# Two of three token tiles of a half batch by seven block products instead of eight, with the block sums on GpSimd

## The chip, the cores and the metric

The kernel runs on one core of a Trainium2 chip. The metric is the device time of one execution in microseconds. A core has five engines that work beside each other: TensorE (PE; its weight loads are shown apart as PEld), VectorE (DVE), ScalarE (ACT), GpSimd (POOL) and SyncE (SP), which here only starts transfers.

## The reference

Attention with routing, then a feed-forward layer. Inputs are q, k and v with 4 batches, 8 heads, 768 tokens and 64 dimensions, centroids (8 heads, 16 clusters), w_in (512 x 2048) and w_out (2048 x 512).

```
q_assign = argmax(q_n . c_n);  k_assign = argmax(k_n . c_n)      # q_n, k_n, c_n normalised
scores   = q . k^T / sqrt(64), or -1e9 where q_assign != k_assign
x        = softmax(scores) . v           # heads side by side: (3072, 512)
h        = x @ w_in                      # (3072, 2048)
out      = (h * sigmoid(h)) @ w_out      # (3072, 512), float32
```

## The kernel before, in words

A batch's 768 tokens are split in two half batches (b, c) of 384 tokens, which are three tiles of 128 tokens. Everything is on chip in f16 with sums in f32. Work goes through these steps, and the names are those that the profile shows:

- **Codes.** q and k arrive as f32 (`raw`). VectorE makes a high part of them (`hi`, L122) and the rest (`lo`, L127) as f16 in `hl`; the transpose of it is `ab`. TensorE multiplies by the centroids (`psN`, L175), VectorE sums and finds the largest (`lsum` L187, `mx_n` L203) and marks it (`ge_n`, L212). The marks become extra rows of `ab` that make scores of different clusters vanish: over TensorE (`psC`) and a copy for early jobs, for late ones over GpSimd (L219, L220), a transposing transfer, and a transfer that GpSimd issues (`c_move`, L232).
- **Scores.** `qk_mm` (L343): two matmuls of 384 columns into `pS`, which has two buffers. `exp` on ScalarE (L348) makes `P`. There are 192 such units.
- **Values.** v arrives as `vn`, GpSimd casts it into `vt` (L290) beside a column of ones. `pv` (L360): 36 matmuls of 65 columns into `pO` for two heads of a half batch; the 65th column is the sum. `norm` on VectorE (L370, L372) divides; the result `xn` is transposed into `xt`.
- **First layer, unit a.** For each of the 16 blocks of 128 of the 2048 features, four matmuls of 384 columns into `ph` (L410), tanh on ScalarE (L430) and the gate `(tanh + 1) * h` on VectorE (L433), which writes `gt`: silu(h) times two. The last half batch makes part of them in pairs (`unit_aa`, `phs`, L448).
- **Second layer, part b.** For each tile of 128 tokens, 16 matmuls of 512 columns over the 16 feature blocks, `gt` as weights and `wout_s` as the moving operand, into `po` (L468), in four groups of four. VectorE halves the result into `ot` (L475), SP sends it out.

PSUM has eight banks: two buffers of two banks for `pS`, and four banks from one free list for `ph`, `pO`, `psN`, `psC`, `px` and `po`. A bank is free again when the copy or gate that reads it is done.

The order of all instructions is fixed when the program is built. The start-up is a list written by hand (`plan`), which also makes the first 8 blocks of the first half batch. After it a planner with a clock for each engine takes, step by step, the piece that can start first; pieces have set lengths and ranks, scores are spaced by `PACE`, and a half batch's output comes while the next one's first layer and scores are interleaved with it. The last half batch (3, 1) has an order of its own at the end, and its last tile is made in three column pieces (L986, L992).

Of the kernel before, what the change touches and what calls it, by code (L numbers as in the profile page):

```python
# [34 lines left out]
def kernel(  # L35
# [54 lines left out]
    zz = const.tile([128, 512], f16, name="zz")  # L90
# [11 lines left out]
    def load(job, eng=nc.sync):  # L102
        raw = mp.tile([128, 12, D], f32, name="raw", tag="raw", bufs=8)
# [122 lines left out]
    def c_xpose(job):  # L226
        cd = cds[job.name] = mp.tile([128, 2, 128], f16, name="cdt", bufs=4)
        nc.sync.dma_start_transpose(cd, ohd[nn[job.name] % 3].rearrange("p h n -> p (h n)"))  # L228
# [54 lines left out]
    def load_v(i, eng=nc.sync):  # L283
        vn = mp.tile([128, NJ, D], f32, name="vn", bufs=5)
        eng.dma_start(vn.rearrange("p j d -> p (j d)"), v[i // H, i % H].rearrange("(p j) d -> p (j d)", j=NJ))
        vns[i] = vn
# [59 lines left out]
    def exp(u):  # L346
        P = mp.tile([128, 2, HALF], f16, name="P", bufs=16)
# [18 lines left out]
    def norm(i, c):  # L366
# [4 lines left out]
        xn = mp.tile([128, 2 * NM, D], f16, name="xn", bufs=3)  # L371
# [49 lines left out]
    def unit_a_end(b, c, fb, ph):  # L421
# [7 lines left out]
        def tanh():  # L429
            nc.scalar.activation(out=tn, in_=ph[:, 0:HALF], func=AF.Tanh, bias=0.0, scale=0.5)  # L430
# [12 lines left out]
    def unit_aa(b, c, fb):  # L443
# [8 lines left out]
        def act():  # L452
            tn = mp.tile([128, 2, HALF], f32, name="tn2", tag="raw", bufs=8)
            nc.scalar.activation(out=tn, in_=ph[:, :, 0:HALF], func=AF.Tanh, bias=0.0, scale=0.5)
# [8 lines left out]
    def part_b(b, c, t, n, bk=3):  # L463
# [9 lines left out]
        def act():  # L473
            ot = mp.tile([128, DM], f32, name="ot", bufs=3)
            nc.vector.tensor_scalar(out=ot, in0=po, scalar1=0.5, scalar2=None, op0=ALU.mult)  # L475
# [3 lines left out]
        return act  # L479

# [14 lines left out]
    def fill(n, bk=3):  # L495
        if n:
            junk = bank("junk", n=bk)
            for _ in range(n):
                nc.tensor.matmul(junk, zz[:, 0:128], zz, start=True, stop=True)
# [11 lines left out]
    for vt in vtb:  # L511
        nc.vector.memset(vt[:, :, D : D + 1], 1.0)
    fill(8)
    nc.gpsimd.memset(hf, 0.5)
    chl = mp.tile([128, 4, D], f16, name="chl")
# [46 lines left out]
    def first(op, n, eng, banks):  # L562
# [96 lines left out]
        evq1.A evk1.D mx0 ge0 hi4.A tr2.13 evq2.A L1.2 hi3.P ct0.03 lo4 mx1 ge1 xr0 cm1 ctk0 hi5.P evk2.A lo5 ctq0  # L659
        tr4.10 ce1.A qk0 hi7.P evk4.A lo3 L2.3 evq4.A tr5.21 mx2 evk5.D ge2 qk1 ex0 qk2 evq5.A w0 lo7 L4.0 vl1 ex1 mx4  # L660
        cm2 tr3.12 ex2 ce2.A xr1 qk3 evq3.D evk3.A qk4 hi6.P tr7.32 ge4 lo6 cm4 L3.1 evq7.D xh0.P ex3 qk5 vl2 evk7.D
# [33 lines left out]
    PACE, LEAST, GAIN = 1.40, 12, .03  # L695
    HOLD = 6

# [23 lines left out]

    dates = {}
# [6 lines left out]
    def chain(job, b):  # L729
        def split(t):  # L730
# [4 lines left out]
            add("DVE", t, 0.5, lambda: hi(job), lambda t: add("DVE", t, 0.9, lambda: lo(job), turned, 1.5), 1.5)  # L735
# [19 lines left out]
        def out_of_bank(t):  # L755
            add("DVE", t + 0.2, 0.44, lambda: cd_ev(job, "D"), lambda t: known(max(clock["SP"], t) + 1.0), 0.3)
# [31 lines left out]
    for i in range(H, B * H):  # L788
# [8 lines left out]
        date(p, lambda t, i=i: cast(i, t))  # L797
    for od in ohd:
# [9 lines left out]
    turn, po_on = 0, None  # L808
# [6 lines left out]
    def norm_piece(n, t):  # L815
# [10 lines left out]
        def after(t):  # L826
            if by_dma(n):
                add("SP", t, 1.28, lambda: xn_d(i, c), lambda t: ready(lands(t, 0.61) + 1.5))
            else:
                tensor_todo.append((t + 0.06, 0.17, lambda: xn_t(i, c), lambda t: add("DVE", t + 0.2, 0.3, lambda: xn_ev(i, c, "D"), ready)))  # L830

        add("DVE", t + 0.2, 0.72, lambda: norm(i, c), after)

    def unit_piece():
# [3 lines left out]
        def gated(t):  # L838
            gate_at[b, c, fb] = t

        def then(t):
            add("ACT", t + 0.2, 0.42, act.tanh, lambda t: add("DVE", t + 0.1, 0.5, act.gate, gated))
            if fb == NFB - 1:
                qb.extend((b, c, t_, n) for t_ in range(NM) for n in range(4))
# [7 lines left out]
    def part_piece():  # L852
        nonlocal po_on
        it = qb.pop(0)
        f = part_b(*it, None)
        po_on = it[:3] if it[3] < 3 else None

        def then(t):
            if f:
                add("DVE", t + 0.2, 0.62, f, sent)  # L860

        return then

    def options(t):
# [3 lines left out]
        if unit < NU and unit - 2 in exp_at and 6 * pv_next > unit - 15:  # L868
            i, c, m = units[unit]
            jn = {qc[i, c][0].name, kt[i, 2 * m][0].name}  # L870
            if all(j in code_at for j in jn):
                r = max([exp_at[unit - 2]] + [code_at[j] for j in jn])

                stock = 1.302 * len(qa) + 0.863 * len(qb) + 20.8 * (unit // 24 - released)
                due = t >= scored + min(max(PACE + GAIN * (stock - LEAST - 0.867 * (24 - unit % 24)), 0.8), 2.2)
# [9 lines left out]
        if qb and (po_on or bank_at is not None):  # L885
            b, c, t_, n = qb[0]
# [135 lines left out]
```

## Time and profile before

| | |
|---|---|
| time, median of 3 runs | 304.73 us (304.69 to 304.85) |
| profiled execution | span 302.8 us from its first to its last instruction; 1.9 us of the median lie around the span |
| TensorE | 294.3 us busy, 97% |
| ScalarE | 211.2 us, 70% |
| VectorE | 200.6 us, 66% |
| GpSimd | 69.1 us, 23% |
| second layer's matmuls of 512 columns (L468) | 368, mean 379 ns each |
| first layer's matmuls of 384 columns (L410) | 480, mean 326 ns each |
| copies of a tile out of PSUM (L475) | 23, mean 688 ns |

A matmul's duration in the profile includes its way through the array, in which the next one already runs; what a group costs TensorE is the distance to the next group's start, and the chain of waits, in order of time, shows groups by that distance. The rows of a view by stage give, for each stretch of time, the busy time of each engine in it.

### The profile page before, as it was taken

The numbers are of one execution on the slowest core, as the hardware profiler recorded it, in microseconds if no ns is written. First come the engines' busy times: TensorE is split into PE (matmuls) and PEld (weight loads), VectorE is DVE, ScalarE is ACT, GpSimd is POOL, SyncE is SP. The second block draws the span as 40 slices with busy tenths as digits, with TensorE's granted clock in tenths as the row PEclk, the third lists the DMA queues.
The fourth block names the chain that finished last, engine by engine and source line by source line (L and its number), as shares of the span: only waits on it lengthen the run. The fifth ranks groups of instructions, "written<-read, shape, count | busy, mean of one in ns | idle before, by whom it ended". The sixth has DMA issues, their size and how long they took to land.

```text
span 302.8 us, 7783 instructions
## 1 busy us (share of the span) xinstructions
PE 294.3 (97%) x3113; PEld 186.3 (62%) x3113; DVE 200.6 (66%) x427; ACT 211.2 (70%) x341; POOL 69.1 (23%) x131
## 2 busy tenths in 40 slices
PE   7899989999999999999999999999999999999995
PEld 3777756566675566655666556655666556755644
DVE  5987669699995679855889468873464136522732
ACT  5899889653985688955698468955897568951520
POOL 2984700101310141433333324122100000000000
PEclk9999999999999999999999999999999999999999
DMA  7888999999794879869999998953101120010102
GB/s 212 249 185 183 201 254 209 247 252 223 174 184 117 218 188 151 197 160 176 231 187 226 187 179 211 163 82 97 38 0 55 46 82 13 16 50 35 37 35 69
DMA packets 74387, 44.07 MB, mean 146 GB/s; under 512 B 54352, under 2 KB 69360, under 8 KB 74352
## 3 DMA queue, kind: packets, MB, share of 16 engines
q1 hardware_dynamic: 69264, 35.16, 50.8%
q0 software_dynamic: 4800, 8.13, 14.2%
q8 instruction: 24, 0.39, 0.6%
q10 hardware_dynamic: 288, 0.30, 0.3%
q14 instruction: 11, 0.09, 0.1%
HBM read 27.30 MB, written 6.29 MB: 111 GB/s over the span
## 4 chain that ended last, share of the span: by engine, by line
PE 87%; ACT 4%; DVE 4%; DMA 2%; SPq 1%; issue 1%; DVEq 0%; ACTq 0%
PE ph L410 25%; PE po L468 25%; PE pS L343 19%; PE pO L360 11%; PE psN L175 3%; ACT P L348 3%; PE phs L448 2%; DVE hl L127 1%; PE po L986 1%; DMA raw<-in_k_dram 1%; DMA xt<-xn 1%; SPq L107 1%; ACT ab L159 1%; PE px L382 0%; SPq L228 0%
## 5 line engine op out<-in xcount | busy, mean ns | idle before, releaser
L348 ACT ACTIVATE P<-pS 128x768 f16<-128x768 f32 x192 | 155.6, 821 | 55.1 <-PE pS L343 54.7
L343 PE MATMUL pS<-ab 128*128 128x384 f16 x384 | 93.2, 326 | 0.5 <-ACT P L348 0.4
L410 PE MATMUL ph<-xt,win_s 128*128 128x384 f16 x480 | 92.4, 326 | 1.2 <-DVE gt L433 0.8
L468 PE MATMUL po<-wout_s,gt 128*128 128x512 f16 x368 | 90.8, 379 | 0.0
L433 DVE SCALAR_TENSOR_TENSOR gt<-tn,ph 128x384 f16<-128x384 f32 x120 | 64.0, 549 | 23.7 <-ACT tn L430 23.1
L430 ACT ACTIVATE tn<-ph 128x384 f32<-128x384 f32 x120 | 60.1, 507 | 10.1 <-PE ph L410 8.1
L410 PEld LDWEIGHTS <-win_s 128*128 128x128 f16 x480 | 46.2, 98 | 31.4 <-issue 2.0
L468 PEld LDWEIGHTS <-gt 128*128 128x128 f16 x368 | 35.0, 98 | 33.8
L343 PEld LDWEIGHTS <-ab 128*128 128x128 f16 x384 | 34.7, 98 | 26.1 <-issue 1.1
L360 PEld LDWEIGHTS <-P 128*128 128x128 f16 x1152 | 39.8, 97 | 4.4
L360 PE MATMUL pO<-vt,P 128*128 128x65 f16 x1152 | 41.2, 193 | 0.0
L127 DVE SCALAR_TENSOR_TENSOR hl<-raw,hl 128x768 f16<-128x768 f32 (+3 forms) x35 | 31.9, 916 | 0.8 <-ACT hl L118 0.4
L475 DVE TENSOR_SCALAR ot<-po 128x512 f32<-128x512 f32 x23 | 15.8, 688 | 23.3 <-PE po L468 23.1
L290 POOL CAST vt<-vn 128x384 f16<-128x384 f32 x32 | 17.9, 558 | 46.4 <-DMA vn<-in_v_dram 41.9
L187 DVE TENSOR_REDUCE L<-psN 128x192 f32<-128x384 f32 (+1 forms) x27 | 14.9, 550 | 15.1 <-PE psN L175 15.0
L232 POOL DMA_DIRECT2D ab<-cdt x16 | 8.9, 557 | 58.0 <-PE pS L343 28.0
L175 PEld LDWEIGHTS <-ab 128*128 128x128 f16 x458 | 17.2, 97 | 5.0 <-DMA ab<-hl 1.1
L175 PE MATMUL psN<-stk,ab 128*128 128x32 f16 (+1 forms) x458 | 18.6, 188 | 0.5 <-DMA ab<-hl 0.5
L370 DVE RECIPROCAL zr<-pO 128x6 f32<-128x6 f32 x32 | 6.2, 193 | 19.2 <-PE pO L360 18.8
L372 DVE TENSOR_TENSOR xn<-pO,zr 128x384 f16<-128x384 f32 x32 | 17.8, 557 | 1.1
L219 POOL TENSOR_SCALAR od<-od 128x96 f16<-128x96 f16 x16 | 9.2, 576 | 36.0 <-DVE od L212 35.9
L122 DVE TENSOR_SCALAR hl<-raw 128x768 f16<-128x768 f32 x24 | 13.9, 580 | 0.6 <-DMA raw<-in_k_dram 0.6
(75 smaller groups left out, 155.8 us busy)
## 6 DMA issues: line engine op xcount, KB each, us to landing
raw<-in_k_dram SPq DMA_DIRECT2D x31, 192.0 KB, 3.8
out_dram<-ot SPq DMA_DIRECT2D x23, 256.0 KB, 2.3
raw<-in_q_dram SPq DMA_DIRECT2D x24, 192.0 KB, 3.6
vn<-in_v_dram SPq DMA_DIRECT2D x16, 192.0 KB, 4.5
vn<-in_v_dram POOLq DMA_DIRECT2D x16, 192.0 KB, 3.7
win_s<-in_moe_w_in_dram POOLq DMA_DIRECT2D x8, 256.0 KB, 6.7
wout_s<-in_moe_w_out_dram POOLq DMA_DIRECT2D x4, 512.0 KB, 18.2
raw<-in_q_dram SPq DMA_DIRECT2D x2, 384.0 KB, 4.3
```

The source lines that it names most:

```text
L127: nc.vector.scalar_tensor_tensor(out=hl[:, s, 1, :], in0=raws[job.name][:, s, :], scalar=QS, in1=hl[:, s, 0, :], op0=ALU.mult, op1=ALU.sub ...
L175: nc.tensor.matmul(L[:, n % g, :, n // g], ab[:, i, :], stk[:, job.groups[i // 3][0], x : x + w], start=(x == 0), stop=(x + w == 2 * HC),)
L290: nc.gpsimd.tensor_copy(vt[:, :, 0:D], vns.pop(i))
L343: nc.tensor.matmul(pS[:, e, 0:HALF], abs_[kj.name][:, kn, :], rhs, start=True, stop=True)
L348: nc.scalar.activation(out=P, in_=pst.pop(u)[:, :, 0:HALF], func=AF.Exp, bias=0.0, scale=ESC)
L360: nc.tensor.matmul(o[:, (2 * t + h) * VW : (2 * t + h + 1) * VW], Ps[i + h, c, j // 2][:, j % 2, ts(t, 128)], vtb[(i + h) % 13][:, j, 0:VW ...
L372: nc.vector.tensor_tensor(out=xn, in0=ov[:, :, 0:D], in1=zr.unsqueeze(2).to_broadcast([128, 2 * NM, D]), op=ALU.mult)
L410: nc.tensor.matmul(ph[:, 0:HALF], win_s[:, r, ts(fb, 128)], xts[b, c][:, r, :], start=(r == 0), stop=(r == NR - 1))
L430: nc.scalar.activation(out=tn, in_=ph[:, 0:HALF], func=AF.Tanh, bias=0.0, scale=0.5)
L433: nc.vector.scalar_tensor_tensor(out=gt[:, fb, :], in0=tn, scalar=1.0, in1=ph[:, 0:HALF], op0=ALU.add, op1=ALU.mult)
L468: nc.tensor.matmul(po, gts[b, c][:, fc, ts(t, 128)], wout_s[:, fc, :], start=(fc == 0), stop=(fc == NFB - 1))
L475: nc.vector.tensor_scalar(out=ot, in0=po, scalar1=0.5, scalar2=None, op0=ALU.mult)
```

## The change

Six of the eight half batches, all but (0, 0) and (3, 1), make their first two tiles' outputs together. The activations of two tiles are seen as a 2x2 block matrix (two tiles by two halves of the 2048 features), and w_out as another (two halves of the features by two halves of the 512 columns). Instead of eight block products there are seven (Strassen's method, in Winograd's order), each of eight matmuls of 256 columns. For this there are

- four sums or differences of blocks of w_out, made once in eight pieces (`tw_piece`), and four of `gt` for each pair of tiles (`sums`; the third and fourth in place), all on GpSimd, each with 1024 columns;
- products that add up in two banks, `X` and `Y`: ScalarE copies `X` after product 1 (`p1`, 256 columns) and after product 5 (`u2`, 512 columns), and VectorE adds (`c11`, `c22` with 256 columns, `c12` with 512).

The order of a pair's products is 1, 2, 6, 5, 7, 4, 3; the third tile follows as before, or in between where a product is not ready. Room for the sums comes from other buffers: raw has 4 instead of 8, and five of the first jobs use the buffers in which the block sums come later; P 12 instead of 16, vn 4 instead of 5, xn 2 instead of 3, cdt 3 instead of 4. The value's column of ones becomes twos, so that x comes out halved, tanh takes h/2 as it is, and the outputs need no factor of a half. The planner's numbers change (`PACE` 1.40 to 1.34, the work of a half batch 20.8 to 20.05), and it may put some copies and some `hi` on ScalarE instead of VectorE (`either`). The warm-up matmuls have 256 columns and are twice as many. In the start-up list the loads xr0 and xr1 stand later.

```diff
-        raw = mp.tile([128, 12, D], f32, name="raw", tag="raw", bufs=8)
+        own = {f"k{n}": f"tw{n}" for n in range(4)} | {"k4": "sg"}
+        tag = own.get(job.name)
+        raw = mp.tile([128, 12, D], f32, name="raw", tag=tag or "raw", bufs=1 if tag else 4)
...
-        P = mp.tile([128, 2, HALF], f16, name="P", bufs=16)
+        P = mp.tile([128, 2, HALF], f16, name="P", bufs=12)
...
+    def tw_piece(n, h):
...
+        a, b_ = (
+            (wout_s[:, ks, up], wout_s[:, ks, lo_]),
+            (wout_s[:, us, up], wout_s[:, ks, up]),
+            (wout_s[:, us, up], tws[0][:, ks, :]),
+            (wout_s[:, us, lo_], tws[2][:, ks, :] if n == 3 else None),
+        )[n]
+        nc.gpsimd.tensor_tensor(out=tws[n][:, ks, :], in0=a, in1=b_, op=ALU.subtract)
...
+        def sums(self, k):
...
+            a11, a12 = gt[:, low, 128:256], gt[:, high, 128:256]
+            a21, a22 = gt[:, low, 0:128], gt[:, high, 0:128]
+            s1, s2 = self.sg[:, 0], self.sg[:, 1]
+            o, x, y, op = (
+                (s1, a21, a22, ALU.add), (s2, s1, a11, ALU.subtract), (a21, a11, a21, ALU.subtract), (a12, a12, s2, ALU.subtract)
+            )[k - 1]
+            nc.gpsimd.tensor_tensor(out=o, in0=x, in1=y, op=op)
+
+        def product(self, k):
...
+            o = self.Y[:, lo_] if k == 2 else self.X[:, up if k in (5, 3) else lo_]
+            for f in range(HK):
+                if k in (5, 6):
+                    w, x = self.sg[:, k - 5, f, :], tws[0 if k == 5 else 2][:, f, :]
+                else:
+                    fc = f if k in (1, 7) else HK + f
+                    w = gt[:, fc, 0:128] if k in (4, 7) else gt[:, fc, 128:256]
+                    x = tws[3 if k == 4 else 1][:, f, :] if k in (4, 7) else wout_s[:, fc, up if k == 3 else lo_]
+                nc.tensor.matmul(o, w, x, start=(f == 0 and k in (1, 2)), stop=(f == HK - 1), skip_group_check=True)
+
+        def p1(self):
+            self.ot = mp.tile([128, DM], f32, name="ot", bufs=3)
+            nc.scalar.activation(out=self.ot[:, HD:DM], in_=self.X[:, 0:HD], func=AF.Copy, bias=0.0, scale=1.0)
+
+        def c11(self):
+            nc.vector.tensor_tensor(out=self.ot[:, HD:DM], in0=self.Y[:, 0:HD], in1=self.ot[:, HD:DM], op=ALU.add)
+            done(self.Y)
+
+        def u2(self):
+            nc.scalar.activation(out=uu[:, HD : HD + DM], in_=self.X, func=AF.Copy, bias=0.0, scale=1.0)
...
+        def c22(self):
+            nc.vector.tensor_tensor(out=self.ot[:, 0:HD], in0=self.X[:, 0:HD], in1=uu[:, DM : DM + HD], op=ALU.add)
...
+        def c12(self):
...
+            nc.vector.tensor_tensor(out=ot, in0=self.X, in1=uu[:, 0:DM], op=ALU.add)
+            done(self.X)
...
-    PACE, LEAST, GAIN = 1.40, 12, .03
+    PACE, LEAST, GAIN, WORK = 1.34, 12, .03, 20.05
...
+    for n in range(8):
+        date(42 + n, lambda t, n=n: add("POOL", t, 2.6, lambda: tw_piece(n // 2, n % 2)))
...
+    paired = {(b, c) for b in range(B) for c in range(2)} - {(0, 0), (B - 1, 1)}
...
+        names = {6: ("c1", "s2"), 5: ("s1",), 7: ("u2", "s3"), 4: ("c22",), 3: ("c22", "s4")}[n]
```

The planner books 2.6 us for each sum on GpSimd. In the changed kernel the products' matmuls stand at L536, the sums of weights at L502 and those of activations at L520.

188 lines of the change are left out of this document (149 added, 39 removed).

## The prediction

> **What bounds the kernel now.** I read the page first, then busy time by stage, then the chain of waits in order of time.
>
> ```profile
> span 302.8 us, 7783 instructions
> PE 294.3 (97%) x3113; PEld 186.3 (62%) x3113; DVE 200.6 (66%) x427; ACT 211.2 (70%) x341; POOL 69.1 (23%) x131
> PE   7899989999999999999999999999999999999995
> PE 87%; ACT 4%; DVE 4%; DMA 2%; SPq 1%; issue 1%; DVEq 0%; ACTq 0%
> ```
>
> TensorE is busy nearly throughout and carries 87% of the chain that ended last. A busy TensorE could still be one that waits inside its pipeline, so the next view is the chain's own pieces, where a group of matmuls lasts as long as it holds up the next one.
>
> ```profile
> 50.11 0.65 PE ph L410 x4
> 52.93 1.09 PE pO L360 x36
> 289.08 6.91 PE po L468 x32
> ```
>
> From these the pitch follows: 0.1625 us for 384 columns (0.65/4), 0.216 us for 512 (6.91/32), 0.030 us for 65 columns with a weight load each (1.09/36). The line through the first two has 0.000416 us per column; at 256 columns it gives 0.109 us.
>
> ```profile
> 40.00:80.00 40.00, 38.90 (x402) 24.42 (x400) 33.56 (x67) 27.37 (x45) 2.54 (x5) 1.00 1.09 229
> 140.00:160.00 20.00, 19.34 (x203) 12.21 (x202) 15.02 (x30) 15.63 (x26) 8.06 (x14) 1.00 1.01 204
> 53.00:75.00 22.00, 21.74 (x256) 13.59 (x253) 18.40 (x39) 11.30 (x16) 2.04 (x4) 1.00 1.12 243
> 89.00:101.00 12.00, 12.00 (x137) 7.44 (x136) 7.46 (x16) 7.35 (x11) 0.00 (x0) 1.00 0.68 160
> 128.00:140.00 12.00, 12.00 (x144) 7.36 (x143) 7.86 (x17) 6.49 (x8) 4.17 (x11) 1.00 0.74 162
> 164.00:176.00 12.00, 12.00 (x118) 6.77 (x114) 7.48 (x16) 5.68 (x7) 3.96 (x10) 1.00 0.94 198
> 199.00:210.00 11.00, 11.00 (x98) 6.09 (x96) 4.74 (x11) 5.68 (x7) 3.04 (x7) 1.00 0.46 91
> ```
>
> The columns are stretch, length, then busy time of PE, PEld, DVE, ACT and POOL, clock, DMA share, GB/s. From 40 us to 280 us TensorE idles only 1.10 us before 80 and 0.66 us around 150, at clock 1.00. So TensorE work bounds that stage, and work taken from TensorE comes off the end one for one as long as nothing new makes it wait. The last five rows are where the new sums will fall: the output stages of the half batches, and 53 to 75 us for the sums of weights. VectorE idles 4.5, 4.1, 4.5 and 6.3 us in the four output stages, ScalarE 4.7 to 6.3 us, but VectorE only 3.6 us between 53 and 75.
>
> **The change, part by part.**
>
> *TensorE.* Per half batch two tiles cost 32 matmuls of 512 columns, 6.91 us. Now they cost 7 x 8 = 56 of 256 columns: 56 x 0.109 = 6.12 us. Saved: 0.79 us, in six half batches **4.7 us**. The third tile and the half batches (0,0) and (3,1) stay. The warm-up matmuls become twice as many of half the width: 22 instead of 11, 0.05 us more, ahead of the first data. Weight loads go from 32 to 56 per half batch; the 65-column row shows a load and a matmul every 0.030 us, so a load hides under 0.109 us. If it did not, rival four applies.
>
> *Copies out.* Fourteen VectorE copies of a tile go, twelve for good and two to ScalarE; six times come sums of 256, 256 and 512 columns.
>
> ```profile
> L475 DVE TENSOR_SCALAR ot<-po 128x512 f32<-128x512 f32 x23 | 15.8, 688 | 23.3 <-PE po L468 23.1
> L372 DVE TENSOR_TENSOR xn<-pO,zr 128x384 f16<-128x384 f32 x32 | 17.8, 557 | 1.1
> L430 ACT ACTIVATE tn<-ph 128x384 f32<-128x384 f32 x120 | 60.1, 507 | 10.1 <-PE ph L410 8.1
> L348 ACT ACTIVATE P<-pS 128x768 f16<-128x768 f32 x192 | 155.6, 821 | 55.1 <-PE pS L343 54.7
> ```
>
> VectorE loses 14 x 0.69 = 9.7 us and gets 6 x (0.42 + 0.42 + 0.69) = 9.2 us (256 columns from the line through the first two rows): nothing. ScalarE gets 6 x (0.40 + 0.61), two tile copies and two small ones, 8 us (line through the last two rows). I cost that at nothing because of the idle 4.7 to 6.3 us per output stage; without that cover it would be 1 us per half batch.
>
> *Sums on GpSimd.* 24 sums of activations and 8 of weights, each 128x1024 of two f16 inputs. No row shows this operation.
>
> ```profile
> L290 POOL CAST vt<-vn 128x384 f16<-128x384 f32 x32 | 17.9, 558 | 46.4 <-DMA vn<-in_v_dram 41.9
> L120 POOL TENSOR_SCALAR hl<-raw 128x576 f16<-128x576 f32 x4 | 6.6, 1657 | 3.5 <-DVE hl L127 2.9 <-PE pTq L150 0.5
> L120 POOL TENSOR_SCALAR hl<-raw 128x768 f16<-128x768 f32 x2 | 4.3, 2134 | 1.0 <-DVE hl L127 1.0
> ```
>
> Lowest, one input read as fast as the cast reads: 1024/384 x 0.51 (undisturbed, below) = 1.4 us. Highest, two inputs each as slow as the scaling of L120 (slope 2.48 ns an element): 5.3 us. I take **2.7 us**: the bytes read equal 1024 f32, which L120's slope puts at 2.77, and 2048 elements at the cast's rate are 2.72. All 32 make 86 us beside POOL's 69: half the span, so POOL is no bound as a whole; what counts is when each sum is done. The Trainium skill, "GPSIMD Engine Reference", section "Elementwise — side-by-side cycle accounting", gives 4497 ns for an f32 sum of 2048 elements; half of that, an estimate, is 2.25 us, and the sums would then never be late; no row here shows it.
>
> In the built order of the changed kernel product 6, the third in line, needs the second sum. The first sum starts when the last gate of the half batch is through, about 1.35 us after the pitch of its last ph group ends (0.16 of drain, 0.51 tanh, 0.55 gate, hand-overs). For (0,1) there stand between that ph and product 6: six pS pairs (1.95), two code products (0.22), a pO (1.09), one psN (0.35), two po groups (1.73), two products (1.74), 7.1 us. So two sums fit if one takes at most (7.1 - 1.35)/2 = 2.85. In the same manner, with what other POOL rows stand between, the limits are 3.26, 3.33, 3.24, 3.43 and 2.78 for the other five; for products 7, behind four sums, the tightest is 2.76 in (1,0). At 2.7 nothing waits. At 3.0, which lock waits could make of it in the first stages, (0,1) loses 0.3 and (1,0) 1.0 us. I book 0.5 us.
>
> *A sum that TensorE waits for on VectorE.* Product 4 writes where the 256-column sum c22 reads, directly behind product 7. In (0,1) one pS pair stands between (0.33 + drain against 0.42), in (2,0) a ph group. Any VectorE operation ahead of c22 shows there; half a gate (0.27) in the first, less in the second: 0.4 us. Behind a late c22 queue gates and pO norms, which hold banks.
>
> *The SBUF access that GpSimd and VectorE share.* Here the trace speaks against the change.
>
> ```profile
> 183.58 0.51 POOL L290 CAST vt<-vn 128x384 f16<-128x384 f32 x1
> 183.70 0.82 DVE L122 TENSOR_SCALAR hl<-raw 128x768 f16<-128x768 f32 x1
> 126.68 0.98 DVE L127 SCALAR_TENSOR_TENSOR hl<-raw,hl 128x768 f16<-128x768 f32 x1
> 126.80 1.22 POOL L290 CAST vt<-vn 128x384 f16<-128x384 f32 x1
> ```
> ```profile
> 9.32 1.65 POOL L120 TENSOR_SCALAR hl<-raw 128x576 f16<-128x576 f32 x1 [0.49 <-PE pTq L150]
> 9.39 1.21 DVE L127 SCALAR_TENSOR_TENSOR hl<-raw,hl 128x576 f16<-128x576 f32 x1
> 14.28 0.75 DVE L127 SCALAR_TENSOR_TENSOR hl<-raw,hl 128x576 f16<-128x576 f32 x1
> ```
> ```profile
> L122 DVE TENSOR_SCALAR hl<-raw x24: 549/552/865, 45.4 to 195.8; 128x768 f16<-128x768 f32 x24
> L433 DVE SCALAR_TENSOR_TENSOR gt<-tn,ph x120: 537/548/556, 37.8 to 290.0; 128x384 f16<-128x384 f32 x120
> ```
>
> A cast begun 0.12 us earlier lengthens L122 from 0.55 to 0.82, and a cast begun during L127 takes 1.22 instead of 0.51. But beside the long L120 operation L127 takes 1.21 instead of 0.75, 0.46 more, not the 1.58 that were left of it: the POOL operation held the access 0.53 of its 1.65 us. The gate never waits (537 to 556 ns in all 120). So three VectorE operations are exposed, L122, L127 and L212; in the built order some 15 of them stand beside the sums of weights and 18 beside the sums of (0,1) to (2,0). With sums back to back and a hold h, one of them waits h²/(2 x 2.7) on average. By bytes (0.53 us for 2304, a sum reads 4096) h is 0.94: 0.16 us each, 2.5 us between 53 and 75 against 3.6 idle, 2.9 in the four output stages against 19. I book 1.0 us for unevenness. By elements (2048 against 576) h is 1.88; that is rival two.
>
> *The rest at nothing.* Fewer buffers: for raw 8 become 4 beside five that the sums take over later; the first nine loads still have one each. P 16 to 12: a score unit is issued only while its buffer is free, so scores may run 11 ahead instead of 15; if that cover is too short, TensorE waits for scores in the middle. DMA bytes don't change; the SP queue issues two stores per pair, as before. The start-up, to 40 us, and the tail from (3,1) on keep their order.
>
> *Sum.* 304.73 (median; the profiled execution's span is 302.8, so 1.9 us lie around it and stay) - 4.7 + 0.5 + 0.4 + 1.0 = **301.9 us**, a span of 300.0.
>
> **The rivals.**
>
> *One, sums later than 2.7 us.* The place is TensorE's wait before products 6 and 7; the price follows from the limits above. At 3.15 us product 6 waits 0.6 in (0,1) and 0.7 in (3,0), product 7 0.4 and 1.6 in the first two: 3.3, which ends the gain. At 3.5 it is 8.7: 304.7 - 4.7 + 1.4 + 8.7 = 310. For: the limits are tight, and L120 is a slow POOL operation. Against: both rates near the operation give 2.7.
>
> *Two, the shared access is held longer; slower.* With h = 1.88 the 15 operations beside the sums of weights wait 0.65 each, 9.8 us against 3.6 idle. VectorE becomes the bound there and TensorE waits 6.2 us for norms and sums: 304.7 - 4.7 + 0.9 + 6.2 = 307.1. It decides from h = 1.6. Held for the whole 2.7 us, waits are 1.35 each: 20.3 and 24.3 us, 16.7 and 4.9 over the idle time, some 322. The Trainium skill states this last case as the rule ("SBUF — State Buffer", section "Who interferes with whom": an exclusive lock for the whole instruction). By the cast's rows that holds, by the L120 row it does not. For: nearly all POOL time near 60 us becomes sums. Against: 0.53 of 1.65.
>
> *Three, ScalarE or buffers absorb the gain; about 304.7.* The tanh and exp stages leave ScalarE little, and pairs' products move into them. Against: 70% busy, and the added copies fall mostly into output stages.
>
> *Four, 256 columns cost no less: no gain.* With LDWEIGHTS lasting 98 ns, more loads could show. The 65-column row (0.030 us) speaks against it; 304.7 and a little.
>
> ```profile
> L410 PEld LDWEIGHTS <-win_s 128*128 128x128 f16 x480 | 46.2, 98 | 31.4 <-issue 2.0
> ```
>
> **How the numbers follow.** The forecast has 0.60, own range 299.1 to 303.9: no waits and half of the 1.76 us of old idle time gone at the low end (304.7 - 4.7 - 0.9 = 299.1), 3.9 of waits at the high end. Rival one 0.13, half of it beyond 307; rival two 0.15, 0.05 of that for the hold over the whole instruction; three and four together 0.12. The range 299.1 to 307.2 leaves out about 0.15. A measurement of this kernel tells 0.2% from no change, 0.6 us. Three and four give most of "same"; one and two are slower but for a small part. Faster 0.62, same 0.11, slower 0.27.
>
> **What would show it.** L536 matmuls at a pitch of 0.109 us, seven groups of 0.87 each; POOL's sums at 2.4 to 2.9 us; no TensorE wait before products 6 and 7 over 0.5 us; L122 and L127 counterparts a little longer in mean, and VectorE under 20 of 22 us at 53 to 75. Wrong would be sums over 3.0 us, TensorE waiting on POOL, or VectorE full beside the weights' sums.

## The result and the profile after

The changed kernel takes **312.95 us** (median of 4 runs, 312.35 to 314.66) against 304.71 (4 runs, 304.64 to 304.85): ratio **1.0269** [1.0229, 1.031]. It is slower by 8.2 us, where 2.8 us less was forecast, and the time lies above the whole range. All ratios here, and those of the experiments, are made from undisturbed runs alone, of which one experiment has only three.

The page of the changed kernel, profiled in its slowest run (314.66 us):

```profile
span 312.9 us, 8178 instructions
PE 293.3 (94%) x3268; PEld 202.8 (65%) x3268; DVE 220.3 (70%) x429; ACT 218.7 (70%) x357; POOL 141.5 (45%) x164
PE   6889889949999899989989999999999999999996
PEclk9999999986999999999999999999999999999999
PE 76%; DVE 11%; DMA 6%; issue 3%; ACT 2%; SPq 1%; DVEq 0%; ACTq 0%
```

TensorE carries 76% of the chain instead of 87%, VectorE 11% instead of 4%. TensorE's busy time hardly fell, but one slice in forty holds a 4 and the slice behind it a granted clock of 6 tenths. VectorE's busy time grew by 19.7 us although its copies were exchanged for sums of nearly the same size. What grew are `hi` (6.7 us), `lo` (4.4) and the marks of the codes (9.8), the operations that share the access with GpSimd: an operation that waits for it counts as busy.

First the part that went as forecast. The chain in order of time, from 202 us on, and the GpSimd sums by line, with durations as least, median and greatest in ns:

```profile
202.56 0.87 PE po L536 x8
```
```profile
L520 POOL TENSOR_TENSOR sg<-gt x6: 2121/2125/2370, 99.8 to 278.7; 128x1024 f16<-128x1024 f16 x6
```

Eight matmuls of 256 columns cost 0.87 us, 0.109 each. A sum lasts 2.12 us in the median, well under the 2.7 of the forecast; beside VectorE's operations single ones take up to 2.84. No row among the waits shows TensorE waiting on GpSimd.

Then the part that didn't. The stages (stretch, length, busy time of PE, PEld, DVE, ACT and POOL, clock, DMA share, GB/s):

```profile
53.00:75.00 22.00, 17.82 (x168) 10.32 (x167) 18.15 (x25) 10.69 (x15) 14.06 (x9) 0.85 1.18 223
```
```profile
60.00:80.00 20.00, 15.64 (x165) 9.27 (x163) 16.16 (x21) 7.25 (x11) 18.97 (x12) 0.83 1.02 230
140.00:160.00 20.00, 16.65 (x188) 11.85 (x188) 18.14 (x28) 11.63 (x18) 17.69 (x21) 1.00 0.90 181
200.00:280.00 80.00, 80.00 (x845) 55.62 (x843) 43.36 (x85) 63.10 (x104) 25.49 (x25) 1.00 0.27 63
```

TensorE idles 4.36 us between 60 and 80, where the weights' sums fill GpSimd, and 3.35 us between 140 and 160, of which 2.0 stand at a pair's sums (the other 1.4 are the late load told of below). From 200 to 280 it never idles, though the sums of three of the six pairs fall there: by then hardly any `hi` and `lo` are left (the last `hi`, L124, starts at 206.7).

What ended last around 65 us, from the chain in order of time, and GpSimd beside it from the timeline:

```profile
63.29 0.06 DVE om L214
...
64.19 2.49 DVE hl L124
66.70 2.75 DVE hl L129
...
69.59 0.57 DVE xn L374
70.21 0.50 PE px L384 x3
```
```profile
61.93 9.51 POOL L502 TENSOR_TENSOR tw<-wout_s 128x1024 f16<-128x1024 f16 x4
```

Four sums run one behind the other. `hi` (0.55 us alone) takes 2.49 and `lo` (0.95 alone) takes 2.75; the mark L214 before them took 0.98. In the kernel before a mark takes 0.35, least, median and greatest in ns:

```profile
L212 DVE TENSOR_TENSOR om<-L,mxn x11: 326/352/359, 23.2 to 93.5; 128x192 f16<-128x192 f32 x10, 128x160 f16<-128x160 f32 x1
```

Each of the three waited for a sum that was running and got in between two sums, and the operation behind it met the next one. Behind them in VectorE's order stands `xn`, for which TensorE waits 4.2 us. From its waits:

```profile
PE px L384 <- DVE xn L374: 4.2, 1, 4.2
PE ph L412 <- DVE gt L435: 3.6, 3, 2.0
```

The long wait for a gate, 2.0 us, is the same thing at a pair's sums. VectorE's timeline there:

```profile
152.54 1.43 DVE L214 TENSOR_TENSOR od<-L,mxn 128x192 f16<-128x192 f32 x1
153.90 2.48 DVE L124 TENSOR_SCALAR hl<-raw 128x768 f16<-128x768 f32 x1
156.41 0.96 DVE L129 SCALAR_TENSOR_TENSOR hl<-raw,hl 128x768 f16<-128x768 f32 x1
157.29 0.55 DVE L435 SCALAR_TENSOR_TENSOR gt<-tn,ph 128x384 f16<-128x384 f32 x1
```

TensorE's stop has a second price. Stretches of 2 us:

```profile
68.00:70.00 2.00, 0.00 (x0) 0.00 (x0) 1.97 (x3) 0.00 (x0) 2.00 (x2) 0.63 1.01 307
70.00:72.00 2.00, 1.79 (x18) 1.25 (x19) 1.48 (x5) 0.00 (x0) 2.00 (x2) 0.50 0.98 173
...
74.00:76.00 2.00, 2.00 (x10) 0.92 (x9) 0.58 (x2) 0.74 (x2) 2.00 (x2) 0.66 1.00 304
```
```profile
71.16 1.90 PE L470 MATMUL po<-wout_s,gt 128*128 128x512 f16 x4
...
77.25 1.03 PE L470 MATMUL po<-wout_s,gt 128*128 128x512 f16 x4
```

While TensorE stands the granted clock falls to 0.50, at 68.5 us, and stays there for 6.8 us, of which TensorE works some 5: a group of four matmuls takes 1.90 us at 71 us and 1.03 at 77. Over the groups between 70.2 and 76 that makes 2.5 us. This differs from run to run: the mean clocks of the four runs are 0.989, 0.995, 0.989 and 0.995, so by an estimate from these the clock was low only half as long in two of them.

To see where all of it went I sum, over the trace's matmuls, what the distance from one start to the next has beyond the pitch of the prediction's line (0.0027 us and 0.000416 us a column, but at least 0.033 us, since the 65-column row has 0.030): what TensorE loses, by waits or by the clock.

| us lost in | 0-40 | 40-60 | 60-80 | 80-100 | 100-200 | from 200 | sum | last matmul starts |
|---|---|---|---|---|---|---|---|---|
| before | 6.83 | 1.06 | 0.66 | 0.11 | 1.32 | 0.28 | 10.26 | 299.33 |
| after | 9.43 | 1.06 | 7.22 | 0.37 | 6.73 | 0.61 | 25.42 | 309.64 |

15.2 us more are lost and 4.9 less work is done (the last matmul starts 10.3 later; the medians of the runs differ by 8.2). 6.6 us of it lie at the weights' sums: 4.4 of standstill, and most of the rest the slow clock. Of the 6.7 between 100 and 200 us, three standstills that lose 1.3, 2.1 and 0.9 us stand behind a mark, a `hi` or a `lo` that waited for a pair's sum. One of 1.6 at 139.6 us is another thing, a load of `raw` that took 6.6 us to land. The kernel before lost 1.3 in the same stretch, by other waits, so 5.4 are new. 2.6 are lost in the start-up and 0.6 elsewhere.

### The profile page after: what moved, and what is told of

Same layout as the page of the kernel before. It is cut to its first block, busy times and chain, and to the rows that moved or that the text cites. A ratio compares the mean times of both kernels' runs of the same rounds, so it can differ in the third digit from the quotient of the medians.

```text
span 312.9 us, 8178 instructions
## 1 busy us (share of the span) xinstructions
PE 293.3 (94%) x3268; PEld 202.8 (65%) x3268; DVE 220.3 (70%) x429; ACT 218.7 (70%) x357; POOL 141.5 (45%) x164
## 3 DMA queue, kind: packets, MB, share of 16 engines
q0 software_dynamic: 4800, 8.13, 12.9%
## 4 chain that ended last, share of the span: by engine, by line
PE 76%; DVE 11%; DMA 6%; issue 3%; ACT 2%; SPq 1%; DVEq 0%; ACTq 0%
PE ph L412 23%; PE pS L345 17%; PE po L470 11%; PE po L536 10%; PE pO L362 9%; DVE hl L129 3%; PE psN L177 2%; DVE hl L124 2%; DMA raw<-in_k_dram 2%; PE phs L450 2%; DMA ab<-cd 1%; DMA ab<-hl 1%; PE po L1167 1%; DVE mxn L205 1%; DMA raw<-in_q_dram 1%
## 5 line engine op out<-in xcount | busy, mean ns | idle before, releaser
L345 PEld LDWEIGHTS <-ab 128*128 128x128 f16 x384 | 34.8, 98 | 20.9 <-issue 2.6
L470 PE MATMUL po<-wout_s,gt 128*128 128x512 f16 x176 | 45.0, 390 | 1.4 <-DVE gt L435 1.4
L520 POOL TENSOR_TENSOR sg<-gt 128x1024 f16<-128x1024 f16 x6 | 13.0, 2166 | 55.7 <-DVE gt L435 55.6
L129 DVE SCALAR_TENSOR_TENSOR hl<-raw,hl 128x768 f16<-128x768 f32 (+3 forms) x35 | 36.3, 1042 | 1.2 <-POOL hl L122 0.7
L470 PEld LDWEIGHTS <-gt 128*128 128x128 f16 x176 | 17.0, 100 | 18.5 <-issue 3.1
L536 PEld LDWEIGHTS <-gt 128*128 128x128 f16 x240 | 23.1, 98 | 5.9 <-issue 0.6
L124 DVE TENSOR_SCALAR hl<-raw 128x768 f16<-128x768 f32 x24 | 20.6, 860 | 2.3 <-DMA raw<-in_k_dram 2.3
L177 PEld LDWEIGHTS <-ab 128*128 128x128 f16 x458 | 17.8, 98 | 4.0
L536 PE MATMUL po<-wout_s,gt 128*128 128x256 f16 x144 | 18.7, 273 | 0.0
L480 DVE COPY ot<-po 128x512 f32<-128x512 f32 x9 | 6.2, 691 | 16.9 <-PE po L470 16.9
```

What stands on the lines that cost most here:

```text
L124: nc.vector.tensor_scalar(out=o, in0=i, scalar1=QS, scalar2=None, op0=ALU.mult)
L129: nc.vector.scalar_tensor_tensor(out=hl[:, s, 1, :], in0=raws[job.name][:, s, :], scalar=QS, in1=hl[:, s, 0, :], op0=ALU.mult, op1=ALU.sub ...
L177: nc.tensor.matmul(L[:, n % g, :, n // g], ab[:, i, :], stk[:, job.groups[i // 3][0], x : x + w], start=(x == 0), stop=(x + w == 2 * HC),)
L345: nc.tensor.matmul(pS[:, e, 0:HALF], abs_[kj.name][:, kn, :], rhs, start=True, stop=True)
L470: nc.tensor.matmul(po, gts[b, c][:, fc, ts(t, 128)], wout_s[:, fc, :], start=(fc == 0), stop=(fc == NFB - 1))
L536: nc.tensor.matmul(o, w, x, start=(f == 0 and k in (1, 2)), stop=(f == HK - 1), skip_group_check=True)
```

## The experiments

Theory A: a VectorE operation that needs the shared access waits until a running GpSimd sum has ended, and TensorE waits for what is queued behind it on VectorE. Rivals: GpSimd is simply too busy or its sums late; the pairs' products and copies themselves cost the time; the smaller buffers do.

### The sums in quarters

```diff
-        nc.gpsimd.tensor_tensor(out=tws[n][:, ks, :], in0=a, in1=b_, op=ALU.subtract)
+        for e in range(4):
+            nc.gpsimd.tensor_tensor(out=tws[n][:, 4 * h + e, :], in0=a[:, e, :], in1=b_[:, e, :], op=ALU.subtract)
...
-            nc.gpsimd.tensor_tensor(out=o, in0=x, in1=y, op=op)
+            for e in range(0, HK, 2):
+                nc.gpsimd.tensor_tensor(out=o[:, e : e + 2, :], in0=x[:, e : e + 2, :], in1=y[:, e : e + 2, :], op=op)
```

> Each of the 32 sums on GpSimd is made in four instructions of 256 columns; all else as in the changed kernel. Theory A (VectorE's L124, L129 and L214 wait until a running sum has ended, up to 2.1 us each, and TensorE then waits for the norms and code sums queued behind them): a wait is at most about 0.6 us, the stretch 60 to 80 us loses under 2 us of TensorE instead of 7.3, and the time falls from 313 to between 302 and 306. Theory B (the sums themselves come too late for the products, or the new order on TensorE is the cause): the time stays within 1 us of 313, or rises, since four instructions have more fixed cost than one.

Measured: 1.0075 [1.0044, 1.0105]. The same work in quarters gives back most of the loss: 1.45 us instead of 7.22 between 60 and 80.

```profile
60.00:80.00 20.00, 19.01 (x223) 12.05 (x222) 17.12 (x33) 12.09 (x20) 20.00 (x28) 1.00 1.06 236
```

GpSimd is busier here than in the changed kernel (20.00 of 20), TensorE idles 0.99 us, and the clock stays at 1.00. The time expected under theory A was missed, though: 7.3 us more than before are still lost in the profile, spread over 0 to 120 us and 180 to 200. The largest piece of it, 1.8 us at 112, is a wait for the transfer of `ab`.

With only the weights' sums in quarters:

> Only the eight sums of weights are made in four instructions of 256 columns each; the sums of activations stay whole. Theory A: of the some 10 us lost against a stall-free changed kernel the 6.6 us at 60 to 80 us mostly go, 306 to 308. If the sums of activations were the main cause: 311 to 313.

Measured: 1.0056 [1.0023, 1.0089]. 60 to 80 loses 1.69; at the pairs' whole sums L129 again takes 2.77 us (at 93.61) and TensorE loses 1.3 us behind it, and as much at 145.

### Memsets in place of the sums

```diff
-        nc.gpsimd.tensor_tensor(out=tws[n][:, ks, :], in0=a, in1=b_, op=ALU.subtract)
+        nc.gpsimd.memset(tws[n][:, ks, :], 0.0)
...
-            nc.gpsimd.tensor_tensor(out=o, in0=x, in1=y, op=op)
+            nc.gpsimd.memset(o, 0.0)
```

> All 32 sums are replaced by GpSimd memsets of the same tiles, which read nothing: the block sums are left out, so the outputs of the pairs are not the reference's. All other engines keep their instructions in the same order. Theory A: the waits on VectorE go, and the time is that of the order and of the saved TensorE work alone, 300 to 303. Theory B (order on TensorE, ScalarE or buffers): 310 or more.

Measured: 0.9931 [0.9891, 0.997], 303.43 us, just above the range expected. With the pairs' products, copies, buffers and order all in place, the kernel is 2.1 us faster than before. So neither the products nor ScalarE nor the buffers make the loss of 8 us; the sums do. Whether it is their reading or their length this doesn't tell, since a memset takes 0.9 us where a sum takes 2.12; the scalings below do. One row surprised:

```profile
62.71 2.27 DVE L124 TENSOR_SCALAR hl<-raw 128x768 f16<-128x768 f32 x1
```

`hi` waited even for memsets, for two in a row, while `lo` never did (966 ns in the mean, 970 in the kernel before). TensorE still loses 2.1 us between 60 and 80, 1.4 more than before, behind this `hi`.

### The weights' sums alone, in the kernel before

```diff
-        vn = mp.tile([128, NJ, D], f32, name="vn", bufs=5)
+        vn = mp.tile([128, NJ, D], f32, name="vn", bufs=4)
...
-        xn = mp.tile([128, 2 * NM, D], f16, name="xn", bufs=3)
+        xn = mp.tile([128, 2 * NM, D], f16, name="xn", bufs=2)
...
+    def extra(n):
+        ks = slice(4 * (n % 4), 4 * (n % 4) + 4)
+        nc.gpsimd.tensor_tensor(out=scr, in0=wout_s[:, ks, 256:512], in1=wout_s[:, ks, 0:256], op=ALU.subtract)
+
+    for n in range(8):
+        date(42 + n, lambda t, n=n: add("POOL", t, 2.6, lambda: extra(n)))
```

> The kernel before with eight GpSimd sums of 1024 columns added at the place where the changed kernel makes its sums of weights; their result is not used, TensorE's work is unchanged. (Two buffer counts, vn 4 and xn 2, make room.) Theory A: TensorE loses 4 to 7 us near 55 to 80 us, 309 to 312. If GpSimd beside VectorE costs nothing: 304.7.

Measured: 1.0279 [1.0207, 1.035], a little more than expected. Eight sums that nobody uses make the kernel before as slow as the changed one. The two smaller buffers don't: a later run has them, and more, at 1.0014. Its waits, its timeline and its stages show the same place:

```profile
PE px L382 <- DVE xn L372: 4.4, 1, 4.4
```
```profile
63.32 2.48 DVE L122 TENSOR_SCALAR hl<-raw 128x768 f16<-128x768 f32 x1
65.83 2.75 DVE L127 SCALAR_TENSOR_TENSOR hl<-raw,hl 128x768 f16<-128x768 f32 x1
```
```profile
65.00:70.00 5.00, 0.66 (x10) 0.67 (x11) 4.72 (x6) 0.80 (x1) 4.84 (x3) 0.89 0.42 146
70.00:75.00 5.00, 5.00 (x32) 2.50 (x30) 4.06 (x6) 1.62 (x2) 4.92 (x4) 0.77 0.90 227
```

The lost time between 60 and 80 is 8.13 us. The clock falls in the standstill here too, for 3.4 us (0.89 and 0.77 in these two stretches).

### The hold by itself

A kernel of its own, which does none of the reference's work: VectorE starts an operation some 0.15 us after GpSimd has started one.

```diff
+    for dve in (two_inputs, fast_mode):
+        for kind, tok in ((none, F), (sum_1024, F), (sum_4x256, F), (scale_f32, A), (scale_f16, F), (cast_1024, A), (zero_1024, Hh)):
+            for rep in range(2):
+                V.memset(tok[:, 0:1], 0.0)
+                kind()
+                V.tensor_reduce(out=red, in_=zo[:, 0:256], axis=AX.X, op=ALU.add)
+                dve()
```

> A kernel by itself that computes nothing of the reference (zeros go out): a GpSimd operation starts, and some 0.4 us later a VectorE operation with two SBUF inputs (first half) or the L122 form (second half), after nothing, a sum of 1024, four sums of 256, a scaling of 768 f32, a scaling of 1024 f16, a cast of 1024, a memset of 1024. Access held for a whole instruction: VectorE's operation ends its own length after the GpSimd operation ends (four sums: after the first or second of them). Held for the reading alone: after about half of it or a third. The scaling of f32 showed 0.53 of 1.65 us in the kernel before; if that was the rule, the sum should hold 0.9 to 1.9 us.

The timeline: L89 has the form of `lo` (two inputs from SBUF), alone first, then beside a sum, quarters of a sum (eight in this row, four for each of two operations), a scaling of f32, one of f16, a cast and a memset:

```profile
7.18 0.95 DVE L89 SCALAR_TENSOR_TENSOR lo<-raw,hi 128x768 f16<-128x768 f32 x1
...
8.24 2.12 POOL L69 TENSOR_TENSOR Hh<-F,G 128x1024 f16<-128x1024 f16 x1 [7.80 <-DVE F L97]
8.38 2.78 DVE L89 SCALAR_TENSOR_TENSOR lo<-raw,hi 128x768 f16<-128x768 f32 x1
...
14.30 7.19 POOL L74 TENSOR_TENSOR Hh<-F,G 128x256 f16<-128x256 f16 x8 [0.92 <-DVE F L97]
14.46 1.32 DVE L89 SCALAR_TENSOR_TENSOR lo<-raw,hi 128x768 f16<-128x768 f32 x1
...
23.80 2.13 POOL L77 TENSOR_SCALAR Hh<-A 128x768 f16<-128x768 f32 x1 [0.21 <-DVE A L97]
23.97 1.47 DVE L89 SCALAR_TENSOR_TENSOR lo<-raw,hi 128x768 f16<-128x768 f32 x1
...
29.48 2.77 POOL L80 TENSOR_SCALAR Hh<-F 128x1024 f16<-128x1024 f16 x1 [0.21 <-DVE F L97]
29.64 1.69 DVE L89 SCALAR_TENSOR_TENSOR lo<-raw,hi 128x768 f16<-128x768 f32 x1
...
33.62 1.04 POOL L83 CAST Hh<-A 128x1024 f16<-128x1024 f32 x1 [0.19 <-DVE A L97]
33.80 1.67 DVE L89 SCALAR_TENSOR_TENSOR lo<-raw,hi 128x768 f16<-128x768 f32 x1
...
35.55 0.95 POOL L86 MEMSET Hh<- 128x1024 f16 x1 [0.89 <-DVE Hh L97]
35.73 0.94 DVE L89 SCALAR_TENSOR_TENSOR lo<-raw,hi 128x768 f16<-128x768 f32 x1
```

What VectorE's operation lasts beyond 0.95, and the lead of GpSimd's start added, is the hold: 1.83 + 0.14 = 1.97 of the sum's 2.12 us and 0.72 + 0.18 = 0.90 of the cast's 1.04, both all but the last 0.15. Of the f32 scaling's 2.13 us it is 0.52 + 0.17 = 0.69 and of the f16 scaling's 2.77 it is 0.74 + 0.16 = 0.90, a third of each; of the memset nothing. The scaling of L120, from which I took the hold, is the one kind of operation here that lets go early. The form of `hi`, in the second half, waits for a memset too: 1.19 us instead of 0.55.

### A longer operation with a shorter hold

This follows from the last: a GpSimd scaling of 1024 f16 elements lasts 2.77 us, longer than a sum, and holds 0.90.

```diff
-        nc.gpsimd.tensor_tensor(out=tws[n][:, ks, :], in0=a, in1=b_, op=ALU.subtract)
+        nc.gpsimd.tensor_scalar(out=tws[n][:, ks, :], in0=a, scalar1=0.5, scalar2=None, op0=ALU.mult)
...
-            nc.gpsimd.tensor_tensor(out=o, in0=x, in1=y, op=op)
+            nc.gpsimd.tensor_scalar(out=o, in0=x, scalar1=0.5, scalar2=None, op0=ALU.mult)
```

> The changed kernel, with each of the 32 sums replaced by a GpSimd scaling of 1024 f16 elements of the same tile, so the sums are left out and the pairs' outputs are not the reference's; every other instruction and the order on every engine stay. In the measurement of holds by itself such a scaling took 2.77 us, 0.65 longer than a sum, but kept a VectorE operation of two SBUF inputs only 0.74 us, where the sum kept it 1.8. Theory A (what VectorE is kept from counts, not how long GpSimd is busy): the hold is then the 0.94 us of my forecast; TensorE loses under 3.5 us at 60 to 80 where the changed kernel lost 7.3, nothing over 1 us in any slice from 100 on, and the time is 303.5 to 306, near the 303.4 with memsets. Rival B (GpSimd's length counts, by sums that come late or by the queue behind them): 2.77 us is longer than 2.12, the waits grow, and the time is 313 or more. If 60 to 80 still loses 5 us or more at holds of 0.7 us, the serial chain alone, and not the length of the hold, makes the loss.

Measured: 0.9985 [0.9955, 1.0015], 304.74 us. (The 0.74 us in the expectation is the wait, 1.69 less 0.95; with the lead it is the 0.9.)

```profile
60.00:80.00 20.00, 18.83 (x220) 11.79 (x219) 17.21 (x32) 11.61 (x19) 20.00 (x9) 1.00 1.05 234
```
```profile
L129 DVE SCALAR_TENSOR_TENSOR hl<-raw,hl 128x768 f16<-128x768 f32 x26 | 27.4, 1053 | 0.4
L124 DVE TENSOR_SCALAR hl<-raw 128x768 f16<-128x768 f32 x24 | 16.4, 685 | 0.0
```

GpSimd is full between 60 and 80, as in the changed kernel, yet TensorE loses 1.90 there and not 7.22. The changed kernel's rows for the same two groups:

```profile
L129 DVE SCALAR_TENSOR_TENSOR hl<-raw,hl 128x768 f16<-128x768 f32 x26 | 29.0, 1114 | 0.4
L124 DVE TENSOR_SCALAR hl<-raw 128x768 f16<-128x768 f32 x24 | 20.6, 860 | 2.3 <-DMA raw<-in_k_dram 2.3
```

Here the rival (GpSimd's length counts) is refuted: longer operations, 3% less time. Their length shows once: one product waits 0.7 us for a scaling, near 176 us. The hold is about the one on which the forecast rested, and the time is 304.7, 2.8 us above the forecast. What is lost beyond the kernel before even with that hold is 2.0 us in the start-up (before 40 us), 1.2 and 1.3 at 60 to 80 and 80 to 100, and 0.9 at that product.

### The buffers and the start-up

P with 12 buffers in the kernel before, scores at most 11 ahead:

```diff
-        P = mp.tile([128, 2, HALF], f16, name="P", bufs=16)
+        P = mp.tile([128, 2, HALF], f16, name="P", bufs=12)
...
-        if unit < NU and unit - 2 in exp_at and 6 * pv_next > unit - 15:
+        if unit < NU and unit - 2 in exp_at and 6 * pv_next > unit - 11:
```

> The kernel before with P 12 instead of 16 and scores allowed 11 ahead, nothing else. In the changed kernel, and in all runs of it so far, TensorE waits about 1.0 us near 31 us for a ScalarE exp, which needs a P buffer that a group of pO matmuls later in the hand-written order frees. If the smaller P is the cause: 1.0 to 1.5 us slower than before. If the wait came from the sums or other buffers: no difference.

Measured: 1.0013 [0.9984, 1.0041]. The profile has a wait that the kernel before lacks:

```profile
PE pS L343 <- ACT P L348: 1.1, 2, 1.0
```

The scores wait 1.0 us near 31 us for a buffer of P, in this kernel as in the changed one; the 1.0 to 1.5 us expected in the time don't show beyond the interval.

Then all that the change does to the start-up and to the buffers, without pairs and sums:

```diff
-        raw = mp.tile([128, 12, D], f32, name="raw", tag="raw", bufs=8)
+        own = {f"k{n}": f"tw{n}" for n in range(4)} | {"k4": "sg"}
+        tag = own.get(job.name)
+        raw = mp.tile([128, 12, D], f32, name="raw", tag=tag or "raw", bufs=1 if tag else 4)
...
-        evq1.A evk1.D mx0 ge0 hi4.A tr2.13 evq2.A L1.2 hi3.P ct0.03 lo4 mx1 ge1 xr0 cm1 ctk0 hi5.P evk2.A lo5 ctq0
+        evq1.A evk1.D mx0 ge0 hi4.A tr2.13 evq2.A L1.2 hi3.P ct0.03 lo4 mx1 ge1 cm1 ctk0 hi5.P evk2.A lo5 xr0 ctq0
```

> The kernel before with all that the change does to the start-up and nothing else: raw 4 and five single buffers, P 12 with scores at most 11 ahead, vn 4, xn 2, cdt 3, 22 warm-up matmuls of 256 columns, the loads xr0 and xr1 later. No sums, no pairs. Theory S (the start-up is a cost of its own, from fewer buffers and later loads, which every kernel with the change's buffers has paid): TensorE loses 1.5 to 3 us more than before in the first 40 us, with a wait for a P buffer near 31 us, and the time is 306 to 308, 0.3 to 1.0% above the kernel before. Rival (the losses before 40 us come and go with the landing of the first transfers, whatever the buffers): within 0.2% of the kernel before, as with P alone (1.0013).

Measured: 1.0014 [0.9991, 1.0037], undecided between the two. The profile loses 8.12 us before 40, 1.3 more than the kernel before's 6.83, less than the expected 1.5 to 3. But the kernel before with eight sums, whose P stays at 16, lost 8.09 there as well. So the start-up's share, 2.6 us in the changed kernel's profile, isn't settled: part is the P wait, and how much comes and goes with the landing of the first transfers stays open.

A mend of that wait was tried with the weights' sums in quarters: pc1, the group of `pO` matmuls that frees the buffer, stands ahead in the start-up list.

```diff
-        qk18 vl8 ex18 xM1 qk19 pe0.D pc1 qk20 nm1 vl9 xs1 pa2.0 ex19 ex20 qk21 pb2 qk22 ex21 pc2 xm1 xg1 ex22 nm2 w6
+        pc1 qk18 vl8 ex18 xM1 qk19 pe0.D qk20 nm1 vl9 xs1 pa2.0 ex19 ex20 qk21 pb2 qk22 ex21 pc2 xm1 xg1 ex22 nm2 w6
```

> The sums of weights in four instructions each, as in the second run, and the pO group pc1 ahead of the exp that needs its P buffer. If the P buffers cost the 1.0 us wait near 31 us: 1 us less than the second run, about equal to the kernel before (ratio 0.999 to 1.004). If not: the second run's 1.0056 again.

Measured: 1.0076 [1.0045, 1.0107] against 1.0056 without it. It didn't help; the scores still wait 0.8 us.

### Fewer pairs, where VectorE is free

Only (2,1) and (3,0), weights' sums from unit 141 on, pc1 ahead:

```diff
-        date(42 + n, lambda t, n=n: add("POOL", t, 2.6, lambda: tw_piece(n // 2, n % 2)))
+        date(141 + n, lambda t, n=n: add("POOL", t, 2.6, lambda: tw_piece(n // 2, n % 2)))
...
-    paired = {(b, c) for b in range(B) for c in range(2)} - {(0, 0), (B - 1, 1)}
+    paired = {(2, 1), (3, 0)}
```

> Seven products only for (2,1) and (3,0), whose sums run after VectorE's last two-input work, with the sums of weights moved there too (and one group of pO matmuls, pc1, moved ahead of an exp in the start list). Theory A, VectorE waiting for the access that a sum holds: nothing waits, the two pairs save 1.6 us, and the time is 1 to 2 us under the kernel before. Rival, the order of products with its two banks or the added copies cost time by themselves: no gain, or a loss after 230 us.

Measured: 1.0026 [1.0003, 1.0049]. In the profile the two pairs lose nothing from 200 us on and the last matmul starts at 299.03, 0.3 before that of the kernel before; the expected gain of 1 to 2 us went into the start-up (1.4 us more lost before 40). The runs are not faster at all.

Four pairs, (1,1) to (3,0), all sums in quarters, weights' sums at every second unit from 84 on:

```diff
+    paired = {(1, 1), (2, 0), (2, 1), (3, 0)}
...
+        date(84 + 2 * n, lambda t, n=n: add("POOL", t, 2.6, lambda: tw_piece(n // 2, n % 2)))
```

> The split sums of 256 columns each, but only four pairs, (1,1) to (3,0), and the weights' sums at one piece every second score unit from unit 84 on instead of one per unit from 42 on. TensorE saves 4 x 0.79 = 3.2 us. Theory A (the loss stands where sums meet VectorE's hi, lo and ge; a hold of a quarter of a sum does little): slices 60 to 100 lose no more than before (1.7 us in all), 100 to 200 lose under 2 us, the start-up loses 1.5 to 2.5 more as in all kernels with these buffers; 304.7 - 3.2 + 1 + 2 = 304.5, between 303.5 and 305.5. Rival B (loss comes with the pairs' products and their copies, wherever they stand): four sixths of the loss of the kernel with all sums split, about the 306.9 of four sixths of its way from 304.7 and a time no better than that of the kernel before.

Measured: 1.0136 [1.0081, 1.0191], over three runs; missed. As theory A had it, 60 to 100 loses 0.87 us, and 100 to 160 0.8. But the start-up of this run loses 10.88 us, with a wait of 2.5 for a transfer, and 160 to 200 loses 3.5:

```profile
PE pS L345 <- DMA ab<-cd: 2.5, 1, 2.5
...
PE po L538 <- POOL sg L522: 1.2, 4, 0.5
```

The last row, which the changed kernel with whole sums lacks, says that sums in quarters come so late that the products wait for them. The loss in the start-up isn't from the pairs, whose first sum starts at 169.6 us.

Three pairs, (2,0) to (3,0), the weights' sums in quarters at the same place, the pairs' sums whole:

```diff
+    paired = {(2, 0), (2, 1), (3, 0)}
```

> The change with three pairs only, (2,0), (2,1) and (3,0), whose sums fall where VectorE has hardly any hi and lo left, and the weights' sums in four instructions of 256 columns each, one piece every second score unit from unit 84 on. TensorE saves 3 x 0.79 = 2.4 us. Theory A: nothing over 0.5 us more than before is lost in any slice from 40 us on; what is left is the start-up's 1.5 to 3; 304.7 - 2.4 + 0.3 + 2 = 304.6, between 303.3 and 305.8. Rival B (the split sums come too late for the products, which wait for each, as in the kernel with four split pairs): only if the pairs' sums were split, so not here; it would show as TensorE waiting for GpSimd before a product for over 0.5 us.

Measured: 1.0044 [1.0005, 1.0083]; missed again. The start-up loses 1.9 more than before, and 2.06 us go between 120 and 140. There the timeline of VectorE, and GpSimd beside it:

```profile
125.99 2.50 DVE L214 TENSOR_TENSOR od<-L,mxn 128x192 f16<-128x192 f32 x1
128.41 1.72 DVE L124 TENSOR_SCALAR hl<-raw 128x768 f16<-128x768 f32 x1
```
```profile
123.83 4.42 POOL L503 TENSOR_TENSOR tw<-wout_s 128x256 f16<-128x256 f16 x7
```

The mark (0.35 alone) waits 2.15 us, through the quarter that runs and the three behind it: with more sums queued, VectorE doesn't always get in behind the first. The gate that TensorE needs stands behind it. No version tried that makes the sums beats the kernel before.

## Why the prediction was wrong

**TensorE: right.** 0.109 us per matmul of 256 columns and 0.87 per group were measured; 4.7 us were forecast, and 4.9 less work is what the start of the last matmul and the lost time leave. Rival four falls.

**Sums: right in the safe direction.** 2.12 us instead of 2.7. The 0.5 us booked for late sums did not occur: no row shows TensorE waiting for GpSimd. The 0.4 for c22 did: before product 4 TensorE loses 0.2 us at 114.5 and 0.3 at 289.3, until c22 has ended. Rival one falls. The estimate worked out from the Trainium skill's "GPSIMD Engine Reference", section "Elementwise — side-by-side cycle accounting", 2.25 us, was nearer than mine.

**The hold: the step that failed.** "By bytes (0.53 us for 2304, a sum reads 4096) h is 0.94." The hold was worked out from the one scaling row and carried over to another operation. For the sum h is 1.97 of 2.12, all but the end of it, twice the 0.94 and past the point 1.6 from which rival two decides. That the same row counted by elements gave rival two's 1.88 is luck, since the scaling lets go early and the sum doesn't. The cast's rows, which the prediction quoted ahead of it, had it right: a cast gives way only when it is done. Of two rows that disagree, I chose the one that suited the gain. The Trainium skill's rule ("SBUF — State Buffer", section "Who interferes with whom": whoever starts first has the shared pair for the whole instruction) holds here for sums and casts, within 0.15 us; for the scaling the run differs, 0.69 of 2.13, and the measurement decides. That page also says that an operation with two SBUF inputs doesn't contend with a GpSimd instruction that only writes: the trace agrees, 0.94 us beside a memset.

**The price: the second step that failed.** "2.5 us between 53 and 75 against 3.6 idle" set the waits against VectorE's idle time. The rows refute that way of counting: in the changed kernel VectorE is busy 18.15 us of 22 between 53 and 75, less than the 18.40 before, so the sign I gave ("VectorE under 20 of 22") was met, and TensorE still idled 4.2 us there. The sign that failed is `hi` "a little longer in mean": 860 ns instead of 580. The codes' marks, `hi`, `lo` and the normed `xn` stand in one row on VectorE. Three waits behind one another, 0.6 + 1.9 + 1.8 us, outlast the work that TensorE still had, and the idle time comes only while VectorE has nothing to do because TensorE stands. Rival two had the mechanism and the side, but its 307.1 (h of 1.88) and "some 322" were counted the same way; 312.95 lies between. What neither had is the clock behind the standstill, 2.5 us of the 6.6. Even with scalings and their hold of 0.90, 3.3 us more than in the kernel before are lost from 40 us on, where the forecast booked 1.9; so the hold alone doesn't account for the miss.

**Output stages.** "2.9 in the four output stages against 19" idle: 4.4 us were lost at three places from 100 to 200, by the same chain, with a gate at the end of two of them.

**"The rest at nothing": not settled.** ScalarE, copies and the tail cost hardly anything (0.3 us more is lost from 200 us on). The start-up lost 2.6 us more in the profile. With memsets, where only `hi` still waits, the gain was 2.1 us instead of 4.7, and of the 4.0 us more that its profile loses 1.7 lie in the start-up; by the kernel with the change's start-up alone (1.0014) this isn't shown to be the buffers.

## What to carry to other kernels

Before work is given to an idle GpSimd, list which VectorE operations share its SBUF access (here `hi`, `lo` and the marks, never the gates, all 120 of which took 0.53 to 0.56 us) and what stands behind each in VectorE's order: a running sum delays it by all that is left of the sum, however idle both engines look on average. Price such waits along the one chain that TensorE will need next, not against idle time of the stage. Test it cheaply ahead of the rewrite: eight unused sums in the old kernel showed the whole loss.

## What the runs showed of the hardware

- How long GpSimd keeps VectorE out depends on its operation: 1.97 of 2.12 us for a sum of two inputs, 0.90 of 1.04 for a cast, 0.69 of 2.13 and 0.90 of 2.77 for scalings. A memset of 0.95 us keeps out only the one-input form (`hi`, 1.19 us instead of 0.55), not the one with two inputs (`lo`, 0.94).
- GpSimd operations queued back to back are not always separated for VectorE: it waited for two memsets in a row (2.27 us for `hi`) and for four quarters of a sum, the running one included (2.50 us for a mark).
- A standstill of TensorE of 4.2 us brought the granted clock to 0.50 for 6.8 us, one of 4.4 us in the kernel before with eight sums for 3.4 us. It fell 2.5 us after TensorE had stopped in the one and 3.9 us after in the other. The Trainium skill, "TensorE: Matmul & The Clock Gate", section "HAM oscillation — how this bites in real kernels", warns of idle gaps above some 3.4 us. The trace agrees: both standstills are longer, and waits of 1.2 to 2.0 us, between 100 and 160 us, left the clock at 1.00.
